# Decode attention plus squared-ReLU MLP on one core: the last K unit loaded and used before wo and w1, and the way from o to wo's partitions rebuilt

## The chip, the cores and the metric

The kernel runs on one core of one Trainium2 chip. The metric is the device time of one execution in microseconds; the time of a kernel is the median of its runs. TensorE does the matrix products, VectorE, ScalarE and GpSimd the elementwise work and reductions, SyncE issues nearly all loads. Inputs and the output lie in HBM.

## The reference

Two tokens (B = 2, one step each, D = 576) go through a layer norm, then attention over the last 2048 positions of a K/V cache and, beside it, a two-layer MLP with a squared ReLU. Both results are added to the input.

```python
W = min(4096, max(256, Sk // 4))            # 8192 // 4 = 2048; Hq, Dh = 32, 128; Hkv = 16
q = (xn @ wq) per head
k, v = cache[:, :, Sk - W:, :], each K/V head used by two query heads
p = softmax(q . k * Dh ** -0.5)
attn = (p @ v as [B, 1, Hq * Dh]) @ wo
h = xn @ w1 + b1                            # F = 4608
r = relu(h); mlp = (r * r) @ w2 + b2
return x + attn + mlp                       # xn = layernorm(x)
```

All tensors are bf16.

## The kernel before, in words

**Units.** K and V are cut into eight units: unit u is token b = u % 2 and the four K/V heads of group tq = u // 2. A unit's K and its V are 2 MB each and lie in SBUF with 128 partitions (4 heads by 32 stretches of the sequence) and 16 KB in each. K and V units share one pool of six buffers (`kvpool`), in which the large w2 pieces land later too. A new load into the pool waits until the buffer's last reader is done. wq and w1 share two large buffers and one small one; wo has a single buffer, so its second half waits until the first has been used.

**A step** (`step(u)`): TensorE transposes K of unit u in eight groups of four fp32-typed 128x128 transposes into PSUM (`kT_ps`, three banks); ScalarE and VectorE copy the groups out in turn (1024 bf16 columns each). Scores are products of those copies with the block-diagonal queries `qz`, into `sc_ps`. `softmax(u)` takes a maximum over columns on VectorE, over partitions on GpSimd, and an exponential on ScalarE, whose row sums go to `l1`; VectorE transposes the result in 32x32 blocks. Two steps later, inside the transposes of unit u, unit w = u - 2 is finished: `pv_sum(w)`, `pv(w)`, `pv_end(w)`.

**From p to o.** `pv` makes 16 products with V into `o_ps` (128 partitions by four blocks of 128 columns); of the four blocks each partition wants only one, which its place tells. `pv_sum` multiplies the row sums by a 0/1 matrix `same_c` (fp32) and takes the reciprocal `linv`. `pv_end` scales all 512 columns into `o_sb` on VectorE, and its `fin` makes four fp32 products with the selector `sel_o`, which pick the wanted blocks, add up and transpose: `o_ps[:, 0:8]` then holds o of eight heads, with the head's inner dimension on partitions. VectorE copies that to `oG`.

**From o to wo.** wo's rows lie 16 to a partition. `wo_sel(t)` (t is a half of the heads, four units) spreads `oG` by a mask (`rr`) and moves it by 16 small products with slices of `sel` to wo's partitions (`wps`), then copies to `ws`. `wo_acc(t)` makes 32 products with wo's half into `out_ps`, where x, b2 and all but the last pieces of the MLP are summed too.

**MLP.** `mlp_h_start`, five `mlp_h_block` and `mlp_h_end` make the hidden layer (products with w1, ReLU on ScalarE, square on VectorE, transposes); `mlp_x` (rows of w2 loaded by ScalarE's queue, `w2x`), three `mlp_o` and three `mlp_tail` make products with w2. `out_ps` is copied to `part` in four pieces, `fin_sb` adds `tail_ps` and `part`, and one small DMA writes the output.

**Order.** TensorE's instructions keep the order of the program; the other engines' instructions are placed by a scheduler that keeps dependencies. SyncE issues its loads in the program's order, so a load that waits for a buffer holds those behind it. There, after the fifth step (u = 4): V5, wo's first half, three loads of w1, K7; after the next step V6 and V7; after the seventh (u = 6) wo's second half and six loads of w2. On TensorE, after step 6: the sum and PV of unit 5, `wo_sel(0)`, `wo_acc(0)`, the hidden layer, then step 7 (`step(NU - 1, with_pv=False)`), PV of unit 6, `mlp_x`, PV of unit 7, `wo_sel(1)`, `wo_acc(1)`, w2.

Of the kernel before, what the change touches and what calls it, by code (L numbers as in the profile page):

```python
# [8 lines left out]
F32 = mybir.dt.float32  # L9
# [7 lines left out]
def kernel(  # L17
# [72 lines left out]
    DW = Dh // WR  # L90
# [9 lines left out]
    keep = ctx.enter_context(tc.tile_pool(name="keep", bufs=3))  # L100
# [74 lines left out]
    const.tile([P, 120], F32, name="pad_1")  # L175
# [8 lines left out]
    x_sb = const.tile([B, D], BF16, name="x_sb")  # L184
    nc.scalar.dma_start(out=x_sb[:], in_=x2d)
# [24 lines left out]
    ones_b = const.tile([1, MB], BF16, name="ones_b")  # L210
    nc.vector.memset(ones_b[:], 0.0)
    nc.vector.memset(ones_b[:, 0:MB:BS], 1.0)
    sel_b = const.tile([B, MB], BF16, name="sel_b")
    nc.vector.memset(sel_b[:], 0.0)
    nc.vector.tensor_copy(out=sel_b[:, 0:MB:BS], in_=ident[0:B, 0:B])
# [14 lines left out]
    nc.vector.tensor_scalar(out=xn_sb, in0=x_sb[:], scalar1=mv[:, 0:1], scalar2=rstd[:, 0:1],  # L230
# [6 lines left out]
    pro_ps = psum.tile([P, NXN, B], BF16, tag="misc", bufs=2, name="pro_ps")  # L237
    for c in range(NFULL):
        transpose(out=pro_ps[:, c, :], in_=xn_sb[:, c:NFULL * P:NFULL], identity=ident[:B, :B])
    for sg in range(S):  # L240
# [8 lines left out]
    same_c = const.tile([P, P], F32, name="same_c")  # L249
    nc.vector.tensor_copy(out=same_c[:].rearrange("p (a c) -> p a c", c=NC),  # L250
                          in_=own[:].unsqueeze(1).to_broadcast([P, P // NC, NC]))
# [3 lines left out]
    sel_o = const.tile([P, NS, NC], F32, name="sel_o")  # L255
    nc.vector.tensor_tensor(out=sel_o[:], in0=own[:].unsqueeze(1).to_broadcast([P, NS, NC]),
                            in1=in_s[:].unsqueeze(2).to_broadcast([P, NS, NC]), op=ALU.mult)
# [4 lines left out]
    is_h = const.tile([TH, NJJ * 32], BF16, name="is_h")  # L262
    nc.vector.tensor_copy(out=is_h[:].rearrange("p (a h) -> p a h", h=TH),
                          in_=ident[0:TH, 0:TH].unsqueeze(1).to_broadcast([TH, NJJ * 32 // TH, TH]))
    rmask = const.tile([P, WR], BF16, name="rmask")
    MZ = (2 * NC - 1) * DW
    sel = const.tile([P, 2 * MZ + DW], BF16, name="sel")
    nc.gpsimd.memset(sel[:], 0.0)
    with nc.allow_low_precision(reason="sums of one 1 and zeros"):
        nc.vector.tensor_reduce(out=rmask[:], in_=ident[:].rearrange("p (c r) -> p r c", r=WR), axis=AX.X, op=ALU.add)  # L270
        nc.vector.tensor_reduce(out=sel[:, MZ:MZ + DW], in_=ident[:].rearrange("p (c r) -> p c r", r=WR), axis=AX.X,
                                op=ALU.add)

# [12 lines left out]
    for k in range(2):  # L286
        q_ps.append(psum.tile([P, QB], F32, tag="misc", bufs=2, name=f"q_ps_{k}"))
        nc.vector.memset(q_ps[k][:], 0.0)
# [32 lines left out]
    kT_tiles, sc_tiles, pT_tiles, l_tiles, oG_tiles, o_tiles = {}, {}, {}, {}, {}, {}  # L321
# [18 lines left out]
    def scores(u, t):  # L340
        tq, b = divmod(u, B)
        if t == 0:
            sc_tiles[u] = psum.tile([P, NJJ * 32], F32, tag="sc", bufs=2, name=f"sc_ps_{u}")
            matmul(sc_tiles[u][:], lhsT=far_h[:], rhs=is_h[:], start=True, stop=False, skip_group_check=True)
        sc_ps = sc_tiles[u]
        kT = kT_tiles.pop((u, t))[:].rearrange("p (j k c) -> p j k c", k=P, c=2)
        z = QZ * (1 - t)
        for c in range(2):
            for g in range(4):
                matmul(sc_ps[32 * g:32 * (g + 1), :], lhsT=qz[:, tq, b, c, z:z + SR],  # L350
                       rhs=kT[:, :, 32 * g:32 * (g + 1), c], start=False, stop=(t == NT - 1 and c == 1),
                       skip_group_check=True, tile_position=(0, 32 * g))

    def softmax(u):
        sc_ps = sc_tiles[u]
        m1 = work.tile([P, 1], F32, tag="m1", name=f"m1_{u}")
        nc.vector.tensor_reduce(out=m1[:], in_=sc_ps[:], axis=AX.X, op=ALU.max)  # L357
        m2 = work.tile([P, NC], F32, tag="m2", name=f"m2_{u}")
        nc.vector.tensor_scalar(out=m2[:], in0=off[:], scalar1=m1[:, 0:1], scalar2=None, op0=ALU.add)  # L359
        gmax = work.tile([P, NC], F32, tag="gmax", name=f"gmax_{u}")  # L360
        nc.gpsimd.partition_all_reduce(gmax[:], m2[:], channels=P, reduce_op=ReduceOp.max)  # L361
        gown = work.tile([P, NC], F32, tag="gown", name=f"gown_{u}")
        bias = work.tile([P, 1], F32, tag="bias", name=f"bias_{u}")
        nc.vector.scalar_tensor_tensor(out=gown[:], in0=gmax[:], scalar=-scale, in1=own[:], op0=ALU.mult,  # L364
                                       op1=ALU.mult, accum_out=bias[:])
        p_sb = work.tile([P, NJJ * 32], BF16, tag="p_sb", bufs=1, name=f"p_{u}")
        l1 = keep.tile([P, 1], F32, tag="l1", name=f"l1_{u}")
        nc.scalar.activation(out=p_sb[:], in_=sc_ps[:], func=ACT.Exp, bias=bias[:, 0:1], scale=scale,  # L368
                             accum_out=l1[:])
        pT = keep.tile([P, NJJ, SR], BF16, tag="pT", name=f"pT_{u}")  # L370
        nc.vector.transpose(out=pT[:].rearrange("p j r -> p (j r)"), in_=p_sb[:])  # L371
        pT_tiles[u] = pT
        l_tiles[u] = l1

    def pv(u, part, parts):
        n = NJJ // parts
        if part == 0:
            o_tiles[u] = psum.tile([P, NS * Dh], F32, tag="misc", bufs=2, name=f"o_ps_{u}")
# [8 lines left out]
    def pv_sum(u):  # L387
        sc_ps = sc_tiles.pop(u)
        matmul(sc_ps[:, 0:1], lhsT=same_c[:], rhs=l_tiles.pop(u)[:], start=True, stop=True, skip_group_check=True)
        linv = work.tile([P, 1], F32, tag="linv", name=f"linv_{u}")  # L390
        nc.vector.reciprocal(out=linv[:], in_=sc_ps[:, 0:1])
        o_tiles[(u, 0)] = linv

    def pv_end(u):
        tq, b = divmod(u, B)
        o_ps = o_tiles.pop(u)
        o_sb = work.tile([P, NS, Dh], F32, tag="o_sb", name=f"o_sb_{u}")
        nc.vector.tensor_scalar(out=o_sb[:].rearrange("p s d -> p (s d)"), in0=o_ps[:],  # L398
                                scalar1=o_tiles.pop((u, 0))[:, 0:1], scalar2=None, op0=ALU.mult)

        def fin():
            for k in range(NS):
                matmul(o_ps[:, 0:NC], lhsT=o_sb[:, k, :], rhs=sel_o[:, k, :], start=(k == 0), stop=(k == NS - 1),
                       skip_group_check=True)
            if b == 0:
                oG_tiles[tq] = keep.tile([P, NC, B], BF16, tag="oG", name=f"oG_{tq}")
            nc.vector.tensor_copy(out=oG_tiles[tq][:, :, b], in_=o_ps[:, 0:NC])  # L407

        return fin
# [9 lines left out]
    def wo_sel(t):  # L419
        rr = work.tile([P, WR, 2 * NC * B], BF16, tag="rr", bufs=1, name=f"rr_{t}")  # L420
        for i in range(2):
            oG = oG_tiles.pop(2 * t + i)
            nc.vector.tensor_tensor(
                out=rr[:, :, i * NC * B:(i + 1) * NC * B],
                in0=oG[:].rearrange("p h b -> p (h b)").unsqueeze(1).to_broadcast([P, WR, NC * B]),
                in1=rmask[:].unsqueeze(2).to_broadcast([P, WR, NC * B]), op=ALU.mult)
        wps = psum.tile([P, WR, B], F32, tag="misc", bufs=2, name=f"wps_{t}")
        for h in range(2 * NC):
            matmul(wps[:], lhsT=sel[:, MZ - h * DW:MZ - h * DW + P],
                             rhs=rr[:, :, h * B:(h + 1) * B], start=(h == 0), stop=(h == 2 * NC - 1))  # L430
        ws = ws_bufs[t]
        nc.vector.tensor_copy(out=ws[:, :, 0:MB:BS], in_=wps[:])  # L432
        wo_state[t] = ws
# [55 lines left out]
    def mlp_tail(r0, r1):  # L489
        w2_sb = w2_tiles.pop((NG4 - 1, r0))  # L490
        if r0 == 0:
            mlp["out"] = psum.tile([P, OQ], F32, tag="misc", bufs=2, name="tail_ps")
            nc.vector.memset(mlp["out"][:], 0.0)
# [32 lines left out]
    def step(u, with_pv=True):  # L526
        fin = None
        w = u - 2
        with_pv = with_pv and w >= 0
        for g in range(NG):  # L530
            transposes(u, g)
            if with_pv and g == 1:
                pv_sum(w)
# [11 lines left out]
    def pv_all(u):  # L545
        pv_sum(u)
# [16 lines left out]
    b2_sb = const.tile([1, D], BF16, name="b2_sb")  # L563
    nc.scalar.dma_start(out=b2_sb[:], in_=B_b2.rearrange("(o n) -> o n", o=1))
    step(1)
    load_k(4)
    out_acc(sel_b[:], lambda a, z: x_sb[:, a:z], start=True)
    out_acc(ones_b[:, :], lambda a, z: b2_sb[:, a:z])
    for u in range(2, NU - 1):
        step(u)  # L570
        if u + 1 < NU - 1:
            load_v(u + 1)
        if u == 4:
# [3 lines left out]
        if u + 3 < NU:  # L577
            load_k(u + 3)
        if u == 5:
            load_v(NU - 1)  # L580
# [4 lines left out]
    pv_all(NU - 3)  # L585
    wo_sel(0)
    wo_acc(0)
# [3 lines left out]
    step(NU - 1, with_pv=False)  # L591
# [47 lines left out]
```

## Time and profile before

| | us |
|---|---|
| median of 3 runs | 135.18 (134.98 to 137.09) |
| profiled execution, its own time | 136.98 |
| its span | 135.2 |
| TensorE busy in the span | 99.4 |
| VectorE busy | 56.6 |
| ScalarE busy | 46.5 |
| moved by DMA | 53.76 MB, mean 398 GB/s |

The span is from the first to the last instruction that the profiler recorded; 1.8 us of the execution's own time lie around it. A busy time is the sum of an engine's instructions; work that ends in time for its reader costs nothing however long it is. In the lines of the profile, PE is TensorE, PEld its weight loads, DVE VectorE, ACT ScalarE, POOL GpSimd, SPq the issuing of DMAs by SyncE; `L104` is a line of the kernel (a helper that records every matmul, so the tile names tell them apart), and `x8` a count. The granted clock is a share of TensorE's full clock.

### The profile page before, as it was taken

The page shows a single profiled execution, that of the slowest core. Times are in us where ns is not written, and L with a number is a line of the kernel's source. Part 1 is how long each engine was busy: PE and PEld are TensorE (multiplying, and loading weights), DVE is VectorE, ACT ScalarE, POOL GpSimd, SP SyncE. Part 2 cuts the span into 40 slices and gives each one's busy share as a digit, 9 for nine tenths or more (in the row PEclk, how much of TensorE's full clock was granted, in tenths as well). Part 3 has the DMA queues.
Part 4 walks back from the last instruction along what each step waited for, and adds up shares of the span by engine and source line. Part 5 has one row for each costly group of instructions (what it writes and reads, how often), then busy time and mean ns, then how long its engine had stood idle before and what let it go on. Part 6 is the DMA issues. An engine that isn't in the chain of part 4 may idle for free.

```text
span 135.2 us, 2258 instructions
## 1 busy us (share of the span) xinstructions
PE 99.4 (74%) x939; PEld 64.6 (48%) x939; DVE 56.6 (42%) x154; ACT 46.5 (34%) x65; POOL 5.5 (4%) x18
## 2 busy tenths in 40 slices
PE   0067747979759779877897897788529976977980
PEld 0065423455427455545554574554229744454660
DVE  7934405254482565484393574510052446022010
ACT  6714502178275085093372462200032522000000
POOL 7000000010100100100100100100000001000000
PEclk9999975579999999999999999856985599555599
DMA  4999999999999999999999999999999999999800
GB/s 151 393 419 439 441 415 441 417 441 427 431 427 439 422 427 436 417 446 419 431 431 431 436 426 431 425 431 411 441 427 427 436 439 426 408 433 430 325 13 1
DMA packets 4419, 53.76 MB, mean 398 GB/s; under 512 B 531, under 2 KB 662, under 8 KB 1178
## 3 DMA queue, kind: packets, MB, share of 16 engines
q1 hardware_dynamic: 4320, 53.32, 92.9%
q10 hardware_dynamic: 90, 0.31, 0.6%
q8 instruction: 7, 0.11, 0.3%
q14 instruction: 2, 0.02, 0.0%
HBM read 53.62 MB, written 0.00 MB: 397 GB/s over the span
## 4 chain that ended last, share of the span: by engine, by line
DMA 40%; PE 36%; DVE 14%; issue 3%; SPq 2%; ACT 2%; POOL 1%; POOLq 0%; ACTq 0%; DVEq 0%
DMA w_rem<-in_B_w_dram 27%; DMA wq<-in_A_wq_dram 12%; PE kT_ps L107 12%; PE out_ps L104 7%; PE sc_ps L104 7%; PE o_ps L104 6%; DVE kT L338 4%; DVE o_sb L398 2%; PE q_ps L104 2%; DVE m L357 2%; DVE pT L371 1%; SPq L132 1%; DVE qrow L302 1%; SPq L125 1%; DVE hrow L463 1%
## 5 line engine op out<-in xcount | busy, mean ns | idle before, releaser
L107 PE MATMUL kT_ps<-ident_f,k 128*128 128x128 f32 x256 | 41.4, 310 | 7.7 <-DVE kT L338 3.4
L107 PEld LDWEIGHTS kT_ps<-ident_f,k 128*128 128x128 f32 x256 | 32.6, 160 | 20.6 <-DVE kT L338 5.7
L336 ACT COPY kT<-kT_ps 128x1024 bf16<-128x1024 bf16 x32 | 31.5, 1013 | 20.6 <-PE kT_ps L107 20.6
L338 DVE COPY kT<-kT_ps 128x1024 bf16<-128x1024 bf16 x32 | 21.5, 681 | 15.3 <-PE kT_ps L107 15.3
L104 PE MATMUL sc_ps<-kT,qz 128*32 128x512 bf16 x128 | 10.6, 415 | 5.8 <-DVE kT L338 5.6
L368 ACT ACTIVATE p<-sc_ps,bias 128x512 bf16<-128x512 f32 x8 | 5.5, 687 | 23.1 <-DVE gown L364 19.5
L104 PE MATMUL o_ps<-sel_o,o_sb 128*128 128x8 f32 x64 | 9.1, 268 | 2.9 <-DVE o_sb L398 2.9
L104 PEld LDWEIGHTS o_ps<-sel_o,o_sb 128*128 128x128 f32 x64 | 8.8, 214 | 4.8 <-DVE o_sb L398 4.8
L104 PE MATMUL o_ps<-v,pT 128*32 128x512 bf16 x128 | 10.2, 414 | 0.0
L357 DVE TENSOR_REDUCE m<-sc_ps 128x1 f32<-128x512 f32 x8 | 5.5, 691 | 7.6 <-PE sc_ps L104 7.6
L104 PE MATMUL out_ps<-wo,ws 128*17 128x288 bf16 x64 | 8.0, 442 | 0.7 <-DVE ws L432 0.7
L371 DVE STREAM_TRANSPOSE pT<-p 128x512 bf16<-128x512 bf16 x8 | 5.7, 710 | 5.1 <-ACT p L368 5.1
L104 PEld LDWEIGHTS <-qz 128*32 128x32 bf16 x128 | 2.6, 98 | 9.9 <-DVE kT L338 7.2
L361 POOL PARTITION_ALL_REDUCE gmax<-m x8 | 2.9, 366 | 106.4 <-DVE m L359 106.4
L398 DVE TENSOR_SCALAR o_sb<-o_ps,linv 128x512 f32<-128x512 f32 x8 | 6.0, 750 | 2.2 <-PE o_ps L104 1.7
L601 ACT COPY part<-out_ps 17x144 f32<-17x144 f32 x2 | 0.5, 268 | 18.1 <-DVE part L601 18.1
L104 PEld LDWEIGHTS <-xnT 128*2 128x2 bf16 x100 | 3.0, 92 | 7.8 <-issue 6.7
L104 PEld LDWEIGHTS <-ws 128*17 128x17 bf16 x64 | 4.4, 133 | 3.5 <-issue 0.5
L407 DVE CAST oG<-o_ps 128x8 bf16<-128x8 f32 x8 | 1.4, 170 | 10.2 <-PE o_ps L104 10.2
L463 DVE TENSOR_TENSOR hrow<-t 98x384 bf16<-98x384 f32 x3 | 1.6, 556 | 9.6 <-ACT t L462 9.5
L107 PE MATMUL pro_ps<-ident,tmp_x 2*128 2x2 bf16 x6 | 0.5, 174 | 6.6 <-DVE tmp_x L230 6.6
L462 ACT ACTIVATE t<-h_ps 98x384 f32<-98x384 f32 x3 | 1.4, 488 | 11.5 <-PE h_ps L104 11.2
(88 smaller groups left out, 73.6 us busy)
## 6 DMA issues: line engine op xcount, KB each, us to landing
k<-in_A_k_cache_dram SPq DMA_DIRECT2D x8, 2048.0 KB, 16.3
v<-in_A_v_cache_dram SPq DMA_DIRECT2D x8, 2048.0 KB
wo<-in_A_wo_dram SPq DMA_DIRECT2D x2, 2304.0 KB
w<-in_B_w_dram SPq DMA_DIRECT2D x2, 2304.0 KB, 36.0
wq<-in_A_wq_dram SPq DMA_DIRECT2D x2, 2048.0 KB
w<-in_B_w_dram SPq DMA_DIRECT2D x3, 1296.0 KB, 31.3
w_rem<-in_B_w_dram SPq DMA_DIRECT2D x1, 576.0 KB
w<-in_B_w_dram SPq DMA_DIRECT2D x1, 576.0 KB
```

The lines of the kernel that those rows point to most:

```text
L104: tc.keep_in_program_order(nc.tensor.matmul(*a, **k))
L107: tc.keep_in_program_order(nc.tensor.transpose(*a, **k))
L336: nc.scalar.copy(out=kT, in_=kT_ps[:])
L338: nc.vector.tensor_copy(out=kT, in_=kT_ps[:])
L357: nc.vector.tensor_reduce(out=m1[:], in_=sc_ps[:], axis=AX.X, op=ALU.max)
L361: nc.gpsimd.partition_all_reduce(gmax[:], m2[:], channels=P, reduce_op=ReduceOp.max)
L368: nc.scalar.activation(out=p_sb[:], in_=sc_ps[:], func=ACT.Exp, bias=bias[:, 0:1], scale=scale, accum_out=l1[:])
L371: nc.vector.transpose(out=pT[:].rearrange("p j r -> p (j r)"), in_=p_sb[:])
L398: nc.vector.tensor_scalar(out=o_sb[:].rearrange("p s d -> p (s d)"), in0=o_ps[:], scalar1=o_tiles.pop((u, 0))[:, 0:1], scalar2=None, op0=A ...
L407: nc.vector.tensor_copy(out=oG_tiles[tq][:, :, b], in_=o_ps[:, 0:NC])
L462: nc.scalar.activation(out=t1, in_=mlp["ps"][k][0:RB, :], func=ACT.Relu)
L463: nc.vector.tensor_tensor(out=hrow[:, k * HB:(k + 1) * HB], in0=t1, in1=t1, op=ALU.mult)
```

## The change

**Order.** K7 is loaded right after V5, ahead of wo and w1; step 7 follows step 6 with unit 5's PV inside it; V6 and V7 are loaded together after step 5 as before; `wo_sel(0)`, `wo_acc(0)`, the second half of wo, w2 and the hidden layer come after step 7. At the end PV of unit 6, `mlp_x`, PV of unit 7, `wo_sel(1)`, `wo_acc(1)` and w2 stand as they did.

**From p to wo.** The four 128-column blocks of `o_ps` are multiplied by 0/1 columns (`in_s`) and summed on VectorE into `o1`, 128 columns wide, whose 129th column is the row sum that ScalarE's exponential leaves there. One fp32 product per unit with a 0/1 matrix (`of_h`, shifted by half for odd groups) sums o and the row sums and puts them on the partitions that wo wants, into `op_ps`, which collects four units. `wo_sel` then takes the reciprocal of the sums, makes a mask `mk` of it, multiplies and adds over eight columns into `ws`, all on VectorE. `pv_sum`, `oG`, `rr`, `wps` and the selectors for them go.

**Buffers and constants.** PSUM's two banks `misc` become one bank `o` and one `op`; `keep` has two buffers instead of three; x and b2 lie in one tile and enter `out_ps` by one pair of products instead of two; the constant score mask is read from `ident` by a broadcast.

```diff
...
-    keep = ctx.enter_context(tc.tile_pool(name="keep", bufs=3))
+    keep = ctx.enter_context(tc.tile_pool(name="keep", bufs=2))
...
-    x_sb = const.tile([B, D], BF16, name="x_sb")
-    nc.scalar.dma_start(out=x_sb[:], in_=x2d)
+    xb_sb = const.tile([B + 1, D], BF16, name="xb_sb")
+    x_sb = xb_sb[0:B, :]
+    nc.scalar.dma_start(out=x_sb, in_=x2d)
...
-    ones_b = const.tile([1, MB], BF16, name="ones_b")
-    nc.vector.memset(ones_b[:], 0.0)
-    nc.vector.memset(ones_b[:, 0:MB:BS], 1.0)
-    sel_b = const.tile([B, MB], BF16, name="sel_b")
+    sel_b = const.tile([B + 1, MB], BF16, name="sel_b")
...
-    nc.vector.tensor_copy(out=sel_b[:, 0:MB:BS], in_=ident[0:B, 0:B])
+    nc.vector.memset(sel_b[:, 0:MB:BS], 1.0)
+    nc.vector.tensor_copy(out=sel_b[0:B, 0:MB:BS], in_=ident[0:B, 0:B])
...
-    nc.vector.tensor_scalar(out=xn_sb, in0=x_sb[:], scalar1=mv[:, 0:1], scalar2=rstd[:, 0:1],
+    nc.vector.tensor_scalar(out=xn_sb, in0=x_sb, scalar1=mv[:, 0:1], scalar2=rstd[:, 0:1],
...
-    pro_ps = psum.tile([P, NXN, B], BF16, tag="misc", bufs=2, name="pro_ps")
+    pro_ps = psum.tile([P, NXN, B], BF16, tag="o", name="pro_ps")
...
-    same_c = const.tile([P, P], F32, name="same_c")
-    nc.vector.tensor_copy(out=same_c[:].rearrange("p (a c) -> p a c", c=NC),
-                          in_=own[:].unsqueeze(1).to_broadcast([P, P // NC, NC]))
+    HQ = P // 2
+    of_h = const.tile([P, 3 * HQ], F32, name="of_h")
+    nc.gpsimd.memset(of_h[:], 0.0)
+    nc.vector.tensor_copy(out=of_h[:, HQ:2 * HQ].rearrange("p (c q) -> p c q", c=NC),
+                          in_=own[:].unsqueeze(2).to_broadcast([P, NC, HQ // NC]))
...
-    sel_o = const.tile([P, NS, NC], F32, name="sel_o")
-    nc.vector.tensor_tensor(out=sel_o[:], in0=own[:].unsqueeze(1).to_broadcast([P, NS, NC]),
-                            in1=in_s[:].unsqueeze(2).to_broadcast([P, NS, NC]), op=ALU.mult)
...
-    is_h = const.tile([TH, NJJ * 32], BF16, name="is_h")
-    nc.vector.tensor_copy(out=is_h[:].rearrange("p (a h) -> p a h", h=TH),
-                          in_=ident[0:TH, 0:TH].unsqueeze(1).to_broadcast([TH, NJJ * 32 // TH, TH]))
-    rmask = const.tile([P, WR], BF16, name="rmask")
-    MZ = (2 * NC - 1) * DW
-    sel = const.tile([P, 2 * MZ + DW], BF16, name="sel")
-    nc.gpsimd.memset(sel[:], 0.0)
-    with nc.allow_low_precision(reason="sums of one 1 and zeros"):
-        nc.vector.tensor_reduce(out=rmask[:], in_=ident[:].rearrange("p (c r) -> p r c", r=WR), axis=AX.X, op=ALU.add)
-        nc.vector.tensor_reduce(out=sel[:, MZ:MZ + DW], in_=ident[:].rearrange("p (c r) -> p c r", r=WR), axis=AX.X,
-                                op=ALU.add)
-
+    is_h = ident[0:TH, 0:TH].unsqueeze(1).to_broadcast([TH, NJJ * 32 // TH, TH])
...
-        q_ps.append(psum.tile([P, QB], F32, tag="misc", bufs=2, name=f"q_ps_{k}"))
+        q_ps.append(psum.tile([P, QB], F32, tag=("o", "op")[k], name=f"q_ps_{k}"))
...
-    kT_tiles, sc_tiles, pT_tiles, l_tiles, oG_tiles, o_tiles = {}, {}, {}, {}, {}, {}
+    kT_tiles, sc_tiles, pT_tiles, o1_tiles, op_tiles, o_tiles = {}, {}, {}, {}, {}, {}
...
     def transposes(u, g):
...
-            matmul(sc_tiles[u][:], lhsT=far_h[:], rhs=is_h[:], start=True, stop=False, skip_group_check=True)
+            matmul(sc_tiles[u][:], lhsT=far_h[:], rhs=is_h, start=True, stop=False, skip_group_check=True)
...
     def softmax(u):
-        sc_ps = sc_tiles[u]
+        sc_ps = sc_tiles.pop(u)
...
-        l1 = keep.tile([P, 1], F32, tag="l1", name=f"l1_{u}")
+        o1 = keep.tile([P, Dh + 1], F32, tag="o1", name=f"o1_{u}")
...
-                             accum_out=l1[:])
+                             accum_out=o1[:, Dh:Dh + 1])
...
-        l_tiles[u] = l1
+        o1_tiles[u] = o1
...
     def pv(u, part, parts):
...
-            o_tiles[u] = psum.tile([P, NS * Dh], F32, tag="misc", bufs=2, name=f"o_ps_{u}")
+            o_tiles[u] = psum.tile([P, NS * Dh], F32, tag="o", name=f"o_ps_{u}")
...
-    def pv_sum(u):
-        sc_ps = sc_tiles.pop(u)
-        matmul(sc_ps[:, 0:1], lhsT=same_c[:], rhs=l_tiles.pop(u)[:], start=True, stop=True, skip_group_check=True)
-        linv = work.tile([P, 1], F32, tag="linv", name=f"linv_{u}")
-        nc.vector.reciprocal(out=linv[:], in_=sc_ps[:, 0:1])
-        o_tiles[(u, 0)] = linv
-
     def pv_end(u):
...
+        t, i = divmod(tq, 2)
...
-        o_sb = work.tile([P, NS, Dh], F32, tag="o_sb", name=f"o_sb_{u}")
-        nc.vector.tensor_scalar(out=o_sb[:].rearrange("p s d -> p (s d)"), in0=o_ps[:],
-                                scalar1=o_tiles.pop((u, 0))[:, 0:1], scalar2=None, op0=ALU.mult)
+        o1 = o1_tiles.pop(u)
+        for k in range(NS):
+            kw = dict(out=o1[:, 0:Dh], in0=o_ps[:, k * Dh:(k + 1) * Dh])
+            if k == 0:
+                nc.vector.tensor_scalar(scalar1=in_s[:, 0:1], scalar2=None, op0=ALU.mult, **kw)
+            else:
+                nc.vector.scalar_tensor_tensor(scalar=in_s[:, k:k + 1], in1=o1[:, 0:Dh], op0=ALU.mult, op1=ALU.add,
+                                               **kw)
...
-            for k in range(NS):
-                matmul(o_ps[:, 0:NC], lhsT=o_sb[:, k, :], rhs=sel_o[:, k, :], start=(k == 0), stop=(k == NS - 1),
-                       skip_group_check=True)
-            if b == 0:
-                oG_tiles[tq] = keep.tile([P, NC, B], BF16, tag="oG", name=f"oG_{tq}")
-            nc.vector.tensor_copy(out=oG_tiles[tq][:, :, b], in_=o_ps[:, 0:NC])
+            if i == 0 and b == 0:
+                op_tiles[t] = psum.tile([P, B, Dh + 1], F32, tag="op", name=f"op_ps_{t}")
+            z = HQ * (1 - i)
+            matmul(op_tiles[t][:, b, :], lhsT=of_h[:, z:z + P], rhs=o1[:], start=(i == 0 and b == 0), stop=(i == 1),
+                   skip_group_check=True)
...
     def wo_sel(t):
-        rr = work.tile([P, WR, 2 * NC * B], BF16, tag="rr", bufs=1, name=f"rr_{t}")
-        for i in range(2):
-            oG = oG_tiles.pop(2 * t + i)
-            nc.vector.tensor_tensor(
-                out=rr[:, :, i * NC * B:(i + 1) * NC * B],
-                in0=oG[:].rearrange("p h b -> p (h b)").unsqueeze(1).to_broadcast([P, WR, NC * B]),
-                in1=rmask[:].unsqueeze(2).to_broadcast([P, WR, NC * B]), op=ALU.mult)
-        wps = psum.tile([P, WR, B], F32, tag="misc", bufs=2, name=f"wps_{t}")
-        for h in range(2 * NC):
-            matmul(wps[:], lhsT=sel[:, MZ - h * DW:MZ - h * DW + P],
-                             rhs=rr[:, :, h * B:(h + 1) * B], start=(h == 0), stop=(h == 2 * NC - 1))
+        op = op_tiles.pop(t)
+        linv = work.tile([P, B], F32, tag="linv", name=f"linv_{t}")
+        nc.vector.reciprocal(out=linv[:], in_=op[:, :, Dh])
+        mk = work.tile([P, B, NC], F32, tag="mk", name=f"mk_{t}")
+        nc.vector.tensor_tensor(out=mk[:], in0=own[:].unsqueeze(1).to_broadcast([P, B, NC]),
+                                in1=linv[:].unsqueeze(2).to_broadcast([P, B, NC]), op=ALU.mult)
+        om_t = work.tile([P, NS, Dh], F32, tag="o_sb", name=f"om_{t}")
+        om = om_t[:, 0:B, :].rearrange("p b (q r) -> p b q r", r=WR)
+        nc.vector.tensor_tensor(out=om, in0=op[:, :, 0:Dh].rearrange("p b (q r) -> p b q r", r=WR),
+                                in1=mk[:].unsqueeze(3).to_broadcast([P, B, NC, WR]), op=ALU.mult)
...
-        nc.vector.tensor_copy(out=ws[:, :, 0:MB:BS], in_=wps[:])
+        with nc.allow_low_precision(reason="sums of one term and zeros"):
+            nc.vector.tensor_reduce(out=ws[:, :, 0:MB:BS].rearrange("p r b -> p b r"),
+                                    in_=om.rearrange("p b q r -> p b r q"), axis=AX.X, op=ALU.add)
...
-            mlp["out"] = psum.tile([P, OQ], F32, tag="misc", bufs=2, name="tail_ps")
+            mlp["out"] = psum.tile([P, OQ], F32, tag="o", name="tail_ps")
...
-    def step(u, with_pv=True):
+    def step(u):
...
-        with_pv = with_pv and w >= 0
+        with_pv = w >= 0
...
             transposes(u, g)
             if with_pv and g == 1:
-                pv_sum(w)
...
             if with_pv and g == 2:
...
     def pv_all(u):
-        pv_sum(u)
...
-    b2_sb = const.tile([1, D], BF16, name="b2_sb")
-    nc.scalar.dma_start(out=b2_sb[:], in_=B_b2.rearrange("(o n) -> o n", o=1))
+    nc.scalar.dma_start(out=xb_sb[B:B + 1, :], in_=B_b2.rearrange("(o n) -> o n", o=1))
...
-    out_acc(sel_b[:], lambda a, z: x_sb[:, a:z], start=True)
-    out_acc(ones_b[:, :], lambda a, z: b2_sb[:, a:z])
-    for u in range(2, NU - 1):
+    out_acc(sel_b[:], lambda a, z: xb_sb[:, a:z], start=True)
+    for u in range(2, NU):
         step(u)
-        if u + 1 < NU - 1:
+        if u + 1 < NU - 2:
...
+        if u + 3 < NU:
+            load_k(u + 3)
         if u == 4:
             issue_wo(0)
...
                 issue_w1(i)
-        if u + 3 < NU:
-            load_k(u + 3)
...
-            load_v(NU - 1)
+            for v in (NU - 2, NU - 1):
+                load_v(v)
+    wo_sel(0)
+    wo_acc(0)
     issue_wo(1)
...
         issue_w2(*w)
     mlp_h_start()
-    pv_all(NU - 3)
-    wo_sel(0)
-    wo_acc(0)
     for c in range(KC):
...
     mlp_h_end()
-    step(NU - 1, with_pv=False)
     pv_all(NU - 2)
     mlp_x()
     pv_all(NU - 1)
```

## What the change does to the time: the prediction

> **What bounds the kernel now.** I read, in this order: the page's forty slices and DMA queues, then stretches of the tail, then the chain that ended last, then SyncE's timeline.
>
> ```profile
> PEclk9999975579999999999999999856985599555599
> DMA  4999999999999999999999999999999999999800
> q1 hardware_dynamic: 4320, 53.32, 92.9%
> ```
>
> SyncE's queue moves 53.32 MB and the DMA engines are full from the second slice (3.38 us each) to the 37th. All of it has to come in whatever the order, so the stream is a floor; the question is what stands after it. The stretches of the tail (busy time of the engines, granted clock, DMA share, GB/s):
>
> ```profile
> 120.00:122.00 2.00, 1.81 (x16) 1.72 (x16) 0.38 (x2) 0.00 (x0) 0.00 (x0) 0.50 1.01 430
> 127.00:128.00 1.00, 1.00 (x12) 0.59 (x10) 0.00 (x0) 0.00 (x0) 0.00 (x0) 0.51 0.80 304
> 128.00:129.00 1.00, 1.00 (x20) 0.77 (x18) 0.00 (x0) 0.00 (x0) 0.00 (x0) 1.00 0.29 92
> 129.00:130.00 1.00, 1.00 (x22) 0.77 (x18) 0.00 (x0) 0.00 (x0) 0.00 (x0) 1.00 0.03 9
> ```
>
> The stream runs at some 430 GB/s and dies out between 127 and 130 us; I take 129.7 for the last byte's landing. TensorE is still busy at 131, at half clock until 128. The chain says since when it has been late:
>
> ```profile
> 60.38 36.91 DMA w_rem<-in_B_w_dram
> ...
> 97.34 0.36 PE h_ps L104 x4
> ...
> 102.34 5.30 PE kT_ps L107 x24
> ...
> 116.99 1.85 PE o_ps L104 x12
> 118.84 0.03 issue
> 118.87 0.76 DVE o_sb L398
> 119.63 0.04 issue
> 119.67 1.89 PE o_ps L104 x8
> ...
> 122.98 7.57 PE out_ps L104 x81
> ...
> 131.88 0.28 ACT part L601
> 132.19 0.31 DVE fin_sb L607
> ```
>
> After the remainder of w1 has landed (97.3) no DMA stands in the chain: 35 us of compute, in which the eighth unit's transposes and scores (102.3 to 112) come before everything else. So this execution ends on TensorE, 2.5 us (132.19 against 129.7) after the stream. And on SyncE:
>
> ```profile
> 58.22 0.54 SPq L125 DMA_DIRECT2D v<-in_A_v_cache_dram  x1
> 58.81 0.59 SPq L156 DMA_DIRECT2D wo<-in_A_wo_dram  x1
> ...
> 65.12 0.55 SPq L125 DMA_DIRECT2D k<-in_A_k_cache_dram  x1
> ...
> 92.65 0.33 SPq L156 DMA_DIRECT2D wo<-in_A_wo_dram  x1
> ```
>
> The last K load (65.12) goes out behind wo and w1; the second wo (92.65) waits for the first wo's use.
>
> **What the Trainium skill says.** DMA: Bandwidth & Descriptors, Specifications, puts the ceiling of 16 engines at 435 GB/s; the stretches show 420 to 446, so the stream can't be made faster, only kept full. TensorE: Matmul & The Clock Gate, Part 1, says the clock is halved after an idle window and that the window runs freely, so that its phase differs from run to run; the trace agrees on the halving (0.50 in the tail, 1.00 from 128), and the phase is why I don't trust one execution's tail. VectorE: DVE Perf Modes, "Why PSUM operands drop a tier", caps fp32 from PSUM at one element a cycle; the o_sb row (128x512 from PSUM, 750 ns) fits.
>
> **The change, part by part.**
>
> *K7 ahead of wo and w1.* K7 takes K4's buffer, free when step 4's transposes end (63.3), 4.5 us later than now's issue of wo behind V5. wo and the three w1 loads queue behind that wait on SyncE. Outstanding then are K5 (TensorE waits for it until 65.2), V4, K6 and V5: over 6 MB, or 14 us at 430 GB/s. So no gap. V6 and V7 wait for step 5 as now. The second wo waits for wo_acc(0), which moves behind step 7: K6 is waited for until 74.85, a step takes 9.5 us (65.19 to 74.7), step 7 ends near 93.5, wo_acc(0) near 97; the stream gets to wo near 112. Nothing is starved: cost 0, and a gap would cost its own length.
>
> Landings: K7's 2.10 MB is 4.9 us, so w1's remainder lands at 97.3 + 4.9 = 102.2. What follows it is as now in sum: V6 at 107.1, V7 at 112.0, wo (2.36 MB) 117.5, w2 in three of 1.33 MB (3.1 us each) 120.6, 123.7, 126.8, and 1.0 MB of w2's rest (2.4 us) at 129.2. Drawn to the 129.7 above, the last large w2 lands near 127.2.
>
> *TensorE per unit.* Gone: eight records of o_ps<-sel_o (0.96 us at full clock, 1.88 at half) and two for the sums (0.28). New: one fp32 product 128x129, no row for it; nearest are two records of the fp32 transposes at 310 ns, so 0.6, bounded by 0.4 and 1.3 at half clock. I take 0.6 in the steps, 0.8 in the tail. The steps gain 0.6 us each; TensorE waits for K in them (0.49 before 65.19, 0.66 before 74.85), so that is worth nothing.
>
> *VectorE per unit.* Gone: o_sb 0.75, linv 0.16, oG 0.17. New: four multiply-adds over 128 columns from PSUM. From o_sb, 750 - 384/0.96 = 350 ns; the row part<-out_ps, 144 columns, gives 296. I take 0.3 plus 0.05 between dependent ones: 1.4 us for four (1.2 to 1.9). In the steps they lie between copies of kT, +0.3 us under TensorE's work. In the tail they stand before the product, twice.
>
> *wo_sel.* Now oG 0.17, rr 0.42, 16 small products (the last 0.4), ws 0.22: 1.4 us from 121.55 to 122.98. New: reciprocal 0.16, mk 0.17, a 256-column product from PSUM 0.45, a 256-column sum 0.43 (m<-sc_ps has 512 in 0.69), gaps: 1.4. Equal. The first is put by the scheduler into step 5 on VectorE, where kT's last copy waits some 0.8 us behind it; the K wait of 0.66 covers most.
>
> *Constants, one bias product less, the score mask read from ident with a broadcast:* under the load of wq, which ends at 18.6. 0, at most 0.3.
>
> *The tail, all at half clock:* remainder 102.2; hidden layer 5.0 as now (97.34 to 102.34), 107.2; PV of unit 6 1.9, 109.1; sums 1.4, product 0.8, 111.3; the 16 products with w2x 2.1, 113.4; PV of unit 7 1.9, sums 1.4, product 0.8, 117.5; wo_sel 1.4, 118.9; 32 products with wo 3.7 (122.98 to 126.7), 122.6; two w2 pieces 2.1 each, 126.8. The third lands at 127.2: DMA bound again, by 0.4 us cold and up to 4 us warm. Its 18 products take 1.1 (full clock: 44 in 2.6 us after 128) to 2.1, so 128.3 to 129.3; the four part copies 1.3 (130.89 to 132.19), so 129.6 to 130.6. The last four tail products end at 130.0. fin_sb starts at 130.0 to 130.6 instead of 132.19: 1.6 to 2.2 us less, I take 1.9.
>
> **Sum.** Against its own time the profiled execution goes from 136.98 (span 135.2) to 135.1. The median of the runs shown is 135.18, 1.8 lower, and the profile doesn't show where. If it is the stream, 1.9 holds: 133.3. If it is TensorE's clock in the tail, the median already stands near the floor and 0.2 to 0.4 is left: 134.9. I take between the two, a gain of 1.2: 134.0.
>
> **Rivals.**
> *The median run is on the stream's floor already* (134.9). For: the tail has 13.7 us at 0.50, and two thirds of 1.8 us would come from the warm w2 and PV products alone. Against: the eighth unit's 10 us stay in the chain at any clock.
> *More than 2% faster* (132.2): the median's stream ends earlier in proportion and TensorE stays warm. For: it is the full 2.2 on 135.18 with 0.8 of stream. Against: 0.8 has no source in the change.
> *Slower, TensorE stays the bound* (138.2). Place: between the remainder's landing (102.2, later by 4.9) and wo_acc(1). Price: two sum-and-product pairs cold at their upper bounds (2 x (1.9 + 1.3 - 2.2) = 2.0) and w1's last products cold after their wait (1.0), so wo_acc(1) starts at 121.9. It decides from 119.3 (127.2 less 7.9): past this each us is one at the end. That is 2.6 past it, so 132.6 to 133.2 for fin_sb cold; with the median's warm tail given up, 135.18 + 3 = 138.2. For: the clock falls when TensorE waits, and it will wait more. Against: 32 and 54 products in a row warmed it after 5 us before.
> *It does not do what it says* (K7 stalls the queue): would show as DMA share under 0.9 near 77 us; 14 us of queue speak against it; part of the slower case.
>
> **How the numbers follow.** Forecast 0.45; floor already 0.25; faster 0.15; slower 0.15. A measurement of this kernel tells about 2% from no change, so the first two are both "same": 0.70. Range: the middle cases reach from 133.0 to 135.4; to 132.4 it takes in most of the faster case, to 136.5 half of the slower one.
>
> **What would show it.** Right: K's last issue near 63 and before wo; DMA share near 1 through 125; the chain's last stretch hanging on a w load, with TensorE idle before w2 products; no kT_ps after 95. Part copies near 129 to 130. Wrong: products with wo starting after 119.3 and out_ps solid to the end (slower); a DMA share dip near 77 or 112 (a stall); four adds over 1.9 us; an unchanged lag after the stream.

## The result, and the profile after

The changed kernel takes 134.87 us (median of 4 runs, 134.79 to 134.92). Its ratio to the kernel before is 0.9984, with an interval of 0.996 to 1.0008: no change that can be measured. Its profiled execution takes 134.83 us with a span of 133.0, so that execution is 2.15 us shorter than the profiled one of before (136.98), where the prediction had 1.9, and yet the median has moved by some 0.2. The runs of before in this study reach from 134.65 to 137.96 us, while none of the 36 runs of the changed kernel, e2_order_only and e11_path_filled is above 134.95; the profile of before shown above is of one of its longer runs, and the ratio leaves these out (here it compares with the runs of 134.98 and 135.18 and not with those of 137.09 and 137.44).

The page of the changed kernel, the same slices and queue as for before (a slice is now 3.33 us):

```profile
PEclk9999977999856999999999959999995555555899
DMA  3999999999999999999999999999999999999940
q1 hardware_dynamic: 4320, 53.32, 94.1%
```

The bytes are the same, and the DMA engines stay full from the second slice to the 38th: the new order has opened no gap. TensorE's clock is at half for seven slices near the end, longer than before, and it doesn't matter, as the chain of what ended last says:

```profile
70.42 37.15 DMA v<-in_A_v_cache_dram
...
107.58 22.08 DMA w<-in_B_w_dram
129.67 0.04 issue
129.71 0.27 PE tail_ps L104 x4
...
130.05 0.31 DVE fin_sb L588
```

The 35 us of compute that closed the chain of before are gone. Between 70 and 129.7 us there are only loads, behind them four products and `fin_sb`, at 130.05 instead of 132.19. The stretches of the tail (busy time of PE, PEld, DVE, ACT and POOL, granted clock, DMA share, GB/s):

```profile
120.00:122.00 2.00, 2.00 (x18) 1.23 (x20) 0.00 (x0) 0.00 (x0) 0.00 (x0) 0.50 0.98 413
127.00:128.00 1.00, 0.77 (x14) 0.64 (x15) 0.00 (x0) 0.00 (x0) 0.00 (x0) 1.00 0.74 287
128.00:129.00 1.00, 0.89 (x26) 0.46 (x21) 0.44 (x2) 0.00 (x0) 0.00 (x0) 1.00 0.25 93
129.00:130.00 1.00, 0.59 (x16) 0.24 (x11) 0.15 (x1) 0.53 (x2) 0.00 (x0) 1.00 0.04 14
```

Against before, the right-hand columns are nearly the same (the stream dies out at the same time) and the left ones are not: TensorE had no gap from 127 on and now is idle for a tenth to two fifths of each microsecond. It waits for w2, where it had been late.

### The profile page after: what moved, and what is told of

Read it like the earlier page. It is cut to its first block, busy times and chain, and to the rows that moved or that the text cites. A ratio compares the mean times of both kernels' runs of the same rounds, so it can differ in the third digit from the quotient of the medians.

```text
span 133.0 us, 2059 instructions
## 1 busy us (share of the span) xinstructions
PE 88.9 (67%) x841; PEld 51.4 (39%) x841; DVE 58.4 (44%) x159; ACT 46.6 (35%) x65; POOL 5.4 (4%) x18
## 4 chain that ended last, share of the span: by engine, by line
DMA 83%; PE 9%; ACT 3%; issue 1%; DVE 1%; ACTq 0%; DVEq 0%
DMA k<-in_A_k_cache_dram 33%; DMA v<-in_A_v_cache_dram 28%; DMA w<-in_B_w_dram 17%; PE kT_ps L107 7%; DMA w2x_sb<-in_B_w_dram 5%; PE o_ps L104 1%; ACT L224 1%; ACT kT L323 1%; ACT L190 1%; PE sc_ps L104 1%; DVE kT L325 1%; ACTq L186 0%; ACT L223 0%; DVE fin_sb L588 0%; PE tail_ps L104 0%
## 5 line engine op out<-in xcount | busy, mean ns | idle before, releaser
L107 PE MATMUL kT_ps<-ident_f,k 128*128 128x128 f32 x256 | 40.0, 300 | 11.3 <-DMA k<-in_A_k_cache_dram 5.5
L107 PEld LDWEIGHTS kT_ps<-ident_f,k 128*128 128x128 f32 x256 | 30.5, 152 | 26.2 <-issue 7.1
L104 PE MATMUL o_ps<-v,pT 128*32 128x512 bf16 x128 | 12.9, 504 | 0.0
L384 DVE SCALAR_TENSOR_TENSOR o<-o_ps,in_s,o 128x128 f32<-128x128 f32 x24 | 8.3, 346 | 0.5
L104 PE MATMUL out_ps<-wo,ws 128*17 128x288 bf16 x64 | 6.1, 364 | 1.6 <-DVE ws L417 1.6
L382 DVE TENSOR_SCALAR o<-o_ps,in_s 128x128 f32<-128x128 f32 x8 | 2.7, 341 | 9.9 <-PE o_ps L104 9.9
L104 PE MATMUL h_ps<-w,xnT 128*2 128x384 bf16 x48 | 3.2, 422 | 4.5 <-DMA w<-in_B_w_dram 4.4
L104 PE MATMUL op_ps<-o,of_h 128*128 128x129 f32 x16 | 4.0, 336 | 3.2 <-DVE o L384 3.2
L104 PEld LDWEIGHTS <-hT_sb 128*17 128x17 bf16 (+1 forms) x98 | 4.2, 98 | 3.9 <-issue 2.0
L104 PE MATMUL q_ps<-wq,xnT 128*2 128x512 bf16 x32 | 2.9, 499 | 3.7 <-DMA wq<-in_A_wq_dram 3.7
```

The source lines that it names most:

```text
L104: tc.keep_in_program_order(nc.tensor.matmul(*a, **k))
L107: tc.keep_in_program_order(nc.tensor.transpose(*a, **k))
L382: nc.vector.tensor_scalar(scalar1=in_s[:, 0:1], scalar2=None, op0=ALU.mult, **kw)
L384: nc.vector.scalar_tensor_tensor(scalar=in_s[:, k:k + 1], in1=o1[:, 0:Dh], op0=ALU.mult, op1=ALU.add, **kw)
```

## The experiments

The question is where 2.15 us of a shorter tail went in the median. *The floor*: the runs of before that make up the compared median already end with the stream of loads, so a shorter tail has nothing to give. *A cost given back*: the new order gains on TensorE, and the new path (four sums on VectorE before each product) or a stall takes it away again. *The clock*: before loses its time to half speed in the tail.

### e1_before_again: the kernel before, unchanged, with a profile

> The kernel before, unchanged, profiled once more. Theory A (floor): the executions that make up the median already end on the stream of loads; then, if this execution lies near 135.1, its span is 133.3, the granted clock is 1.00 in most of 103 to 128, TensorE waits for a w load before its last products, and fin_sb starts near 130.3 instead of 132.19. Theory B (two effects that cancel: the order gains about 1%, the new path from o to wo costs about 1%): TensorE is busy without a wait from 123 to 131 here too, and fin_sb starts at 131.5 or later after a stream that ends earlier than 129.7.

134.91 us, span 133.1. The chain that ended last:

```profile
107.00 22.74 DMA w<-in_B_w_dram
129.73 0.04 issue
129.77 0.27 PE tail_ps L104 x4
...
130.12 0.31 DVE fin_sb L607
```

These are the last steps of the changed kernel too, 0.07 us later. Two stretches of the same execution and two lines of its timeline tell why TensorE was in time:

```profile
112.00:116.00 4.00, 2.82 (x38) 2.05 (x38) 1.86 (x6) 0.78 (x2) 0.36 (x1) 1.00 1.01 430
126.00:127.00 1.00, 0.52 (x10) 0.27 (x5) 0.00 (x0) 0.00 (x0) 0.00 (x0) 1.00 0.94 364
```

```profile
115.75 1.05 PE L104 MATMUL o_ps<-v,pT 128*32 128x512 bf16 x16
120.96 3.35 PE L104 MATMUL out_ps<-wo,ws 128*17 128x288 bf16 x32 [0.31 <-DVE ws L432]
```

Here the clock is up when unit 7's PV comes (16 products in 1.05 us, where they took 1.90 in the profile shown of before), and TensorE is idle for half of the microsecond from 126 to 127, before the last large w2 lands. In this execution before is already on the floor, although its clock is down in a part of the tail (0.58 from 116 to 120 us, 0.50 from 120 to 122).

The two profiles of the unchanged kernel also say where the 1.8 us between them lie. They reach the products with `w2x` at the same time (114.39 in the profile shown, 114.36 here). Then the clock is half in one and full in the other: these 16 products take 2.09 and 1.15 us, unit 7's PV 1.90 and 1.05, the products with wo start at 122.98 and 120.96, and `fin_sb` at 132.19 and 130.12. The stream dies out at the same time in both (92 and 109 GB/s from 128 to 129 us, 9 and 10 in the next). So the whole difference between these two executions, 2.07 us, is TensorE's clock in the tail. Why it fell in one and not in the other, the traces don't say.

### e2_order_only and e3_path_only: the two halves of the change

e2 is the kernel before with the new order alone:

```diff
...
-    for u in range(2, NU - 1):
+    for u in range(2, NU):
         step(u)
...
+        if u + 3 < NU:
+            load_k(u + 3)
         if u == 4:
             issue_wo(0)
...
+    wo_sel(0)
+    wo_acc(0)
     issue_wo(1)
...
-    pv_all(NU - 3)
-    wo_sel(0)
-    wo_acc(0)
...
     mlp_h_end()
-    step(NU - 1, with_pv=False)
     pv_all(NU - 2)
```

(two PSUM tiles of the MLP, `ha_ps` and `hb_ps`, move to `misc`, which the order makes necessary). e3 is the changed kernel with this same edit turned round: the new path in the old order.

> The new order alone: K7 ahead of wo and w1, step 7 with the PV of unit 5 before the hidden layer; the path from o to wo is that of before (pv_sum, four products with sel_o, rr, wps), and ha_ps and hb_ps lie in the banks misc, since sc is still in use. Theory A: 134.8 to 135.1, ratio 0.997 to 1.000, the last chain hanging on a w load. Theory B: the order's gain shows without the path's cost, ratio 0.985 to 0.992 (133.2 to 134.1).

> The new path alone: block sums on VectorE, one fp32 product, wo_sel on VectorE, with the order of before (K7 behind w1, step 7 after the hidden layer). Theory A: it shortens TensorE's tail by about 1 us and the stream stays the floor, so 134.8 to 135.2, ratio 0.997 to 1.001. Theory B: its cost shows alone, ratio 1.006 to 1.012 (136.0 to 136.8).

The order alone: 134.82 us, 0.9969 (0.9944 to 0.9994), `fin_sb` at 130.11, the chain on w's load. That is the changed kernel's time, without any of the new path. The path alone: 137.43, 1.0109 (0.9989 to 1.023). Its median is above both cases of the expectation, but the interval includes no change, and its four runs (135.50 to 138.35) largely overlap with those of before in the same comparison (134.65 to 137.68), so the times don't show that it is dearer. Its profiled execution (span 135.7) ends on compute; from its chain:

```profile
119.97 0.36 DVE o L382
...
121.63 0.79 PE op_ps L104 x2
...
123.95 7.14 PE out_ps L104 x81
...
132.73 0.31 DVE fin_sb L589
```

and two of its stretches:

```profile
112.00:116.00 4.00, 0.82 (x6) 0.50 (x2) 2.31 (x8) 0.78 (x2) 0.36 (x1) 0.80 0.99 424
124.00:126.00 2.00, 2.00 (x18) 1.22 (x20) 0.00 (x0) 0.00 (x0) 0.00 (x0) 0.50 1.01 419
```

The softmax of unit 7 and four sums stand one behind the other with nothing for TensorE to do: 0.82 us busy out of 4. The clock then falls, and of the 81 products that follow, from wo to w2, those until 128 run at half clock. But in the profile shown of before the clock falls in the same stretch, with TensorE busy for 2.82 us of it:

```profile
112.00:116.00 4.00, 2.82 (x27) 1.90 (x24) 1.72 (x5) 0.78 (x2) 0.36 (x1) 0.79 0.98 422
```

So the fall can't be put down to the new path alone. Against that profile the path is 1.0 us later at the products with wo (123.95 and 122.98) and 0.5 at `fin_sb` (132.73 and 132.19). *A cost given back* is out for the new order, where the kernel takes the same time with the new path and without it (134.87 and 134.82); in the old order, with step 7 in the tail, it is possible but not shown.

### e4_before_filled and e11_path_filled: keep TensorE's clock up

Both add products that nothing reads (fillers), into columns of the `out_ps` bank that are not copied out: 100 in all to before, 122 to the path alone. The edit, with the counts of e11:

```diff
...
+    def fill(n):
+        for i in range(n):
+            matmul(out_ps[:, OH:OH + P], lhsT=ident[:, 0:32 + MB], rhs=ident[:], start=False, stop=False, ...)
...
+        if u == NU - 1:
+            fill(12)
         scores(u, 1)
...
-        pv_end(u)()
+        fin = pv_end(u)
+        if u > NU - 3:
+            fill(20)
+        fin()
+        if u == NU - 1:
+            fill(20)
...
+        if c == 2:
+            fill(20)
         mlp_h_block(c)
+    fill(30)
     mlp_h_end()
```

> The kernel before with 100 small products (128x49 by 128x128, into unused columns of out_ps's bank) put where TensorE waits after 94 us: 20 before the third block of the hidden layer, 30 after the last, 12 before the second half of step 7's scores, 14 in each of the last two units and 10 before the last wo_sel. They keep TensorE busy, so that its clock should stay at 1.00 in the tail. Theory A: nothing left to gain, 134.8 to 135.3, ratio 0.997 to 1.002, fin_sb at 130.0 to 130.6. Theory B: a faster tail counts in full, ratio 0.985 to 0.992.

> The new path with the order of before, which took 137.43, and 122 small products where TensorE waits after 94 us: 20 before the third block of the hidden layer, 30 after the last, 12 before the second half of step 7's scores, 20 behind the PV of each of the last two units and 20 before the last products with wo. If the path costs time there because TensorE waits on VectorE and so runs at half clock, they take that away: 134.8 to 135.5. If VectorE's four sums themselves are too long for the chain: 136.5 or more.

Before, filled: 135.23, 1.0006 (0.9976 to 1.0036); its profiled execution ends on the stream, `fin_sb` at 130.03. The fillers bring the compared median of before nothing, which speaks against *the clock* as what holds it; its 20 runs reach to 136.60, where those of before reach to 137.68. The path, filled: 134.78, 0.9968 (0.9944 to 0.9992), `fin_sb` at 129.99 behind w's load. All its 20 runs (134.62 to 134.92) lie below the four of the path alone (135.50 to 138.35), and in its trace the clock is 1.00 from 108 us on. So what the path alone had lost to the floor was TensorE's clock and not VectorE's time as such.

### e5_delay_short and e6_delay_long: how much room is there?

Multiplications of `om` by 1.0 in place on VectorE, between `om` and `ws` of the second half, hold back `wo_acc(1)`: four in e5, sixteen in e6.

```diff
+        if t == 1:
+            for _ in range(4):
+                nc.vector.tensor_scalar(out=om, in0=om, scalar1=1.0, scalar2=None, op0=ALU.mult)
```

> The changed kernel with four more in-place multiplications by 1.0 (128x256 fp32 in SBUF) on VectorE ahead of the last sum of wo_sel(1), about 0.25 us each with the gap, so wo_acc(1) starts some 1.0 us later while TensorE waits. Floor theory: in the changed kernel TensorE waited 0.94 us for the last large w2 piece, so nothing is lost: 134.7 to 135.1, beside 134.87. Rival (the last chain runs through VectorE and TensorE after all): the delay counts in full, 135.7 to 136.0.

> The same with sixteen such multiplications, about 4 us of delay of wo_acc(1). Floor theory: the first 0.9 us are free and the rest counts, 4.0 - 0.9 = 3.1, less up to 0.7 from the last products running at full clock behind it: 137.2 to 138.0. Rival: all of it counts, 138.7 to 139.

e5: 134.92, 0.9965 (0.9936 to 0.9994). The products with wo start at 121.20 instead of 120.00, and the median doesn't feel it; in the trace nothing waits for the last large w2 any more, and `fin_sb` starts at 130.35, 0.3 later. e6: 139.16, 1.0257 (1.0183 to 1.0332), above both cases of the expectation, since one multiplication took 0.33 us with its gap and the delay became 5.6 us and not 4. The chain of e6:

```profile
124.96 0.60 DVE ws L420
...
125.61 7.29 PE out_ps L104 x81
...
134.53 0.31 DVE fin_sb L591
```

5.6 us later at `wo_acc(1)` is 4.5 later at `fin_sb` and 4.3 in the median. By the two runs the first 0.9 to 1.3 us of lateness are free, and the rest costs its length. That is the whole margin of the changed kernel in its tail; it waits 0.94 us for the last large w2.

### e7_less_tail and e10_less_tail_filled: take the tail's work away

e7 leaves out `wo_acc(1)` and the products of the first two large w2 pieces; all loads stay. e10 puts 70 fillers in their place, after `wo_sel(1)`.

```diff
...
     wo_sel(1)
-    wo_acc(1)
-    for w in W2P[:NG4 - 1]:
+    fill(70)                      # e10 alone
+    for w in W2P[2:NG4 - 1]:
         mlp_o(*w)
```

> The changed kernel without the 32 products with the second half of wo and the 36 with the first two large w2 pieces; their loads stay. It leaves these terms out of the output, and takes some 6.5 us of TensorE's work out of the tail. Floor theory: nothing changes, 134.7 to 135.0. Rival: TensorE's work is worth something there, 134.3 or less.

> The kernel without the products with the second half of wo and the first two large w2 pieces, and in their place 70 small products that nothing uses. That kernel took 135.67 instead of 134.87, its last 18 products running at half clock behind the last landing. If the idle time ahead of them is what cost 0.8 us, the 70 bring it back: 134.7 to 135.0. If the loss is from elsewhere (the loads, the landing): 135.5 to 135.8 stays.

e7 misses: 135.67 (135.55 to 135.88), 0.8 us above the changed kernel with 6.5 us less for TensorE to do (4.01 and 2.49 in the changed kernel's timeline). e10: 134.79, with 17 of 20 runs under 134.95, so the fillers bring 0.9 us back. From the changed kernel's timeline, then from e7's timeline and its stretches:

```profile
127.23 1.27 PE L104 MATMUL out_ps<-w,hT_sb 128*17 128x288 bf16 x18 [0.94 <-DMA w<-in_B_w_dram]
```

```profile
127.16 1.85 PE L104 MATMUL out_ps<-w,hT_sb 128*17 128x288 bf16 x14 [8.79 <-DMA w<-in_B_w_dram]
```

```profile
128.00:129.00 1.00, 1.00 (x16) 0.64 (x12) 0.00 (x0) 0.00 (x0) 0.00 (x0) 0.50 0.25 92
```

After 8.79 us of idling, the products behind the last large landing run at half clock, with no gap until 130, and `fin_sb` starts at 130.83. The landing is nearly the same, but 14 of these products take 1.85 us in e7 and 18 take 1.27 in the changed kernel: 132 and 71 ns each. In e10 TensorE waits for 3.1 us behind its fillers, and its clock is still 1.00 for the same products. The Trainium skill (TensorE: Matmul & The Clock Gate, "HAM oscillation — how this bites in real kernels") describes this: where a matmul stage is shorter than the wait for its DMA, and the wait is longer than the idle window, the next stage starts throttled (at half clock); here the wait was 8.79 us. It costs 0.8 us of the end. So the work that was hidden ahead of the last landing had a use: it warmed TensorE for what can't be hidden.

### e12_less_load: is the stream the floor?

The changed kernel without the load of the first large w2 piece (1.33 MB) and without its 18 products.

```diff
-    for w in W2P:
+    for w in W2P[1:]:
         issue_w2(*w)
```

> The changed kernel without the first large w2 piece: neither its load (1.33 MB, 3.1 us at 430 GB/s) nor its 18 products; its terms are left out of the output. Floor theory: the stream ends 3.1 us earlier; TensorE, which had 0.9 us to spare and 18 products less, follows within 0 to 0.7: 131.8 to 132.5. Rival (something else sets the end): 134.0 or more.

132.35 (131.86 to 132.37), 0.9806 (0.9777 to 0.9836), 2.5 us less than the changed kernel. Products alone brought nothing when taken away (e7); bytes do: 1.33 MB at the stream's 430 GB/s are 3.1 us. In its profiled execution, the shortest of the four (131.86), w lands at 126.58 instead of 129.67, and `fin_sb` starts at 126.97, 3.08 earlier. *The floor* holds.

### e8_w2x_sixteen and e9_no_w2x: can the end of the stream be improved?

Two attempts to gain on the floor itself. e8 issues `w2x` as two loads on 16 partitions each instead of four on 8; e9 has no `w2x` on ScalarE's queue: SyncE's last three w2 pieces carry all of it, as 6, 2 and 1 rows per partition instead of 4, 2 and 1.

```diff
...
-    XR, XP, XE = 8, 32, 8
+    XR, XP, XE = 8, 32, 16        # e8
...
-    W2P = [(0, 0, 9), (1, 0, 9), (2, 0, 9), (3, 0, 4), (3, 4, 6), (3, 6, 7)]
+    W2P = [(0, 0, 9), (1, 0, 9), (2, 0, 9), (3, 0, 6), (3, 6, 8), (3, 8, 9)]        # e9
...
```

> The changed kernel with the rows of w2 that ScalarE loads in two transfers of 16 partitions instead of four of 8; bytes and products are the same. The DMA share falls from 0.88 to 0.04 between 125 and 130 us, so the engines end unevenly; if the four 8-partition transfers lie on half of the engines (295 KB, 37 KB on each[...]), spreading them over all takes up to 0.7 us off the last landing: 134.1 to 134.4. If the unevenness is from elsewhere: 134.8 to 135.0. If the half with less is the slower one: 135.2 to 135.6.

> The changed kernel without ScalarE's separate transfers of 256 rows of w2: these rows come with the other last rows of w2 on SyncE's queue, 128 partitions wide, in pieces of six, two and one rows; bytes are the same, and the 16 products with K = 32 become eight in the tail. In the kernel with two 16-partition transfers the landings of one load lay closer together (1.7 us instead of 2.9), but the rate fell to 312, 353 and 286 GB/s between 6 and 12 us. If the narrow transfers cost the stream twice, by their place on half of the engines and by that rate, this ends earlier: 133.9 to 134.5. If the last landing is set by engines that are slow anyway: 134.8 to 135.2; the larger last pieces may cost 0.2.

e9: 135.23 (135.08 to 135.47), 1.0009 (0.9991 to 1.0027), w's last landing at 130.06, 0.4 after that of the changed kernel: no gain. e8: 136.14, 1.008 (1.0063 to 1.0096), above all three cases of its expectation. One stretch near its start:

```profile
6.00:8.00 2.00, 0.51 (x6) 0.40 (x6) 1.46 (x6) 0.00 (x0) 0.00 (x0) 1.00 0.97 312
```

From 8 to 10 us it is 353 GB/s at a share of 1.10, from 10 to 12 us 286 at 0.98; the changed kernel has 483, 365 and 483 in these three, at shares of 1.14, 0.85 and 1.13. For the same busy time the DMA engines of e8 move fewer bytes. At the end w lands at 130.5 instead of 129.67; that it is late by what was lost at the start is likely and not shown. Why the rate fell, these runs don't say: besides the shape of the loads, their times differ, since e8 issues all of `w2x` in two loads by 4.8 us and the changed kernel its four at 1.4, 4.8, 27.0 and 35.8. Apart from e12, which leaves a load out, none of the twelve beats the changed kernel and e2 by more than the measurement tells.

## Why the prediction was right or wrong

**The verdict and the path: right.** No change that can be measured was the forecast (0.70), and the measured 134.87 lies in the range; both would have held for 134.0 too. The profiled execution did what the working says: shorter by 2.15 us (1.9), `fin_sb` at 130.05 (130.0 to 130.6), the chain on the last w loads and TensorE idle before them. That the ends agree is no measure of what the change is worth, though: e1 ends 2.07 us ahead of the same profile with no change at all.

**The size: wrong, by the last step of the sum.** The prediction had the end right for the execution it was looking at, saw that the median stood 1.8 us lower, named both explanations (133.3 if the stream sets the median, 134.9 if TensorE's clock in the tail makes the difference), and took "between the two, a gain of 1.2: 134.0". The gain was 0.2 (0.3 against the 135.18 it started from). The step that failed is this middle: it puts a good part of the 1.8 us down to an earlier end of the stream, and the runs show none of that. In e1 the last load lands at 129.73 and in the changed kernel at 129.67, and all of the 2.07 us by which `fin_sb` is earlier in e1 than in the profile of before arise on TensorE behind 114.4 us. A mean of two exclusive explanations is a time that neither gives. Its own rival, *the median run is on the stream's floor already* (134.9), was right, and e1 shows it: the ends of before and after differ by 0.07 us.

The numbers to decide it were there. In the profile of before, 3.0 us lie behind the start of `fin_sb` (135.2 less 132.19) and 1.8 around the span; so the median's `fin_sb` stood near 135.18 - 1.8 - 3.0 = 130.4, inside the 130.0 to 130.6 that the prediction worked out for the floor. What was held against the rival, "the eighth unit's 10 us stay in the chain at any clock", weighed too little: they come ahead of the end, but in e1 TensorE is through with all that it can do 0.86 us before the last large w2 lands.

**K7 costs no stall: right.** K7 is issued at 63.54 (63.3 foreseen) and wo at 64.12; the DMA share is 1.02 from 74 to 78 us and 0.99 from 112 to 116. The second wo goes out at 95.21 (97 foreseen). e2 has the whole order at no cost. The rival that K7 stalls the queue is out.

**The sums and the product: right.** From the changed kernel's timeline, for unit 6:

```profile
109.82 0.35 DVE L382 TENSOR_SCALAR o<-o_ps,in_s 128x128 f32<-128x128 f32 x1 [1.58 <-PE o_ps L104]
110.21 1.12 DVE L384 SCALAR_TENSOR_TENSOR o<-o_ps,in_s,o 128x128 f32<-128x128 f32 x3
111.39 0.80 PE L104 MATMUL op_ps<-o,of_h 128*128 128x129 f32 x2 [1.61 <-DVE o L384]
```

The four sums take 1.51 us from first start to last end (1.4; one takes 0.35 where 0.3 had been taken), the product 0.80 (0.8). `wo_sel` takes 1.5 with its gaps (1.4): 0.17 and 0.17 for the reciprocal and the mask, 0.42 for `om`, and 0.59 for the 256-column sum, where 0.43 had been taken from a row with plain columns.

**The tail's times: right in order, the products with wo 1.1 us too early.** `wo_acc(1)` starts at 120.00 (118.9), the last large w2's products at 127.23 (127.2), and these 18 take 1.27 us (1.1 to 2.1). The difference came out of the 0.4 to 4 us of room the prediction had left before that landing; after it, the measured room (e5, e6) is 0.9 to 1.3.

**The slower rival: not here, but a real one.** Its deciding point was `wo_acc(1)` at 119.3. It started at 120.00 and nothing was lost (the chain ends on the stream), so the point was some 1.6 to 2 us too early: it priced the way from there to the landing at half clock throughout (7.9 us), while the way took 6.3 (123.80 + 2.49 - 120.00), because the clock went up at 124. The Trainium skill (TensorE: Matmul & The Clock Gate, "What's actually happening" in Part 1) lets the throttle go after about 3.4 us of sustained work, at a time that a free-running window decides; TensorE was busy without a gap from 120.00, so it took 4.0 us here. The 4.6 us without a gap from 111.39 to 116.03 had not been enough. e5, whose `wo_acc(1)` starts at 121.20, ended 0.3 us later in its trace and 0.05 in its median. The mechanism itself, TensorE waiting for sums and going on at half clock, can be seen in e3's trace in the old order; that it makes the kernel slower than before isn't shown.

**The faster rival: wrong.** It needed an earlier end of the stream, and the last landing stayed at 129.7.

## What to carry to other kernels

Before a gain in the tail is counted, subtract what is fixed from the median and not only from the profiled execution: if the median less launch and last DMA already stands at the last byte's landing, all that a shorter tail buys is room; here only fewer bytes bought time (e12), and two attempts on the stream itself gained nothing (e8, e9). Two explanations that exclude each other want a choice and a probability, never a number halfway. And leave TensorE something to do ahead of the last landing: what comes after it is paid in full, at the clock that the wait has left.

## What the runs showed of the hardware

Taking 6.5 us of products away ahead of the last landing made the kernel 0.8 us slower (e7), and 70 products that nobody reads took it back (e10). Half clock can hold for 24 us of a working kernel (0.50 from about 100 to 124 in the changed one, TensorE at 2.0 of 2.0 us busy in the stretch shown from 120) while the end still waits for the last load. And DMA engines with a share of 0.97 moved 312 GB/s in e8 where the changed kernel's moved 483 at 1.14, a quarter less for the same share, with only the shape, number and times of one small tensor's loads on another queue changed.
